# Last group of the FFN: three quarters stored over SyncE's and GpSimd's queues, and the last product ordered by token halves

## Chip, cores and metric

The kernel runs on one core of a Trainium2 chip. The metric is the device time of one execution in microseconds. The kernel before takes 313.97 us, the median of three runs (313.96 to 314.85). The profiled execution of it spans 312.5 us from its first to its last instruction, with a granted TensorE clock of 0.999.

## What is computed

A linear attention with cosine weights, then a SwiGLU feed-forward block. Cut to what matters:

```python
# q, k, v: 8 batches x 8 heads x 576 positions x 64
q_p, k_p = phi(q), phi(k)            # relu, times cos and sin of the position: 128 features
num = q_p @ (k_p^T @ v);  den = q_p . sum(k_p) + 1e-6
x = (num / den) as 4608 tokens x 512
out = (silu(x @ w_gate) * (x @ w_val)) @ w_out      # d_ff = 1536, out 4608 x 512, float32
```

## The kernel before

The 4608 tokens go through the feed-forward block in nine groups of 512 (`NTG` = 9, groups 0 to 8). Within a group, the gate and value products fill `ht`, the hidden activations (128 x 12 x 512, fp16), and then `out_by_quarters` (L818) multiplies `ht` by `w_out`. The order of the work is written out by hand (`manual_schedule`): each engine runs its instructions in the order in which they stand in the program, and semaphores hold an instruction until its inputs are there.

**The output product.** `out_by_quarters` computes the 512 x 512 output of a group as four quarters (C11, C12, C21, C22: 256 tokens by 256 columns each) by a scheme with seven products in place of eight. `product` (L835) is one of these: 12 matmuls of 128 x 256, over six blocks `kc` of the contraction and two halves `i` of 128 tokens. In the kernel before, `kc` is the outer loop, so that the two halves alternate and end one matmul apart. In the last group the running sum `b` lies in two PSUM banks, one for each half (`nb = 2 if last else 1`, L856); the helper `copied` (L849) then makes one VectorE instruction for each half. The order at the end of the last group is:

- `product(a, ..)` ends quarter C11; ScalarE scales and copies it into `ob` (L852); `store_two(t0, ..)` (L876).
- `product(b, S1, T1)` ends C22; VectorE adds it into `ob` in two instructions, one for each half (L880); `store_two(t0 + 2, ..)` (L882).
- `product(c, .., T4)` ends C21; ScalarE copies it (L852); `store_two(t0 + 2, ..)` (L887).
- `product(b, S4, ..)` ends C12, the last; VectorE copies it in two instructions (L854); `store` (L896) for each of the two token halves.

**The stores.** `store_two` (L765) writes one quarter with two transfers of 128 KB: `e = 0`, the lower 64 partitions, from SyncE, and `e = 1`, the upper 64, from ScalarE. The last quarter is written by `store` (L759) with four transfers of 64 KB, again one from SyncE and one from ScalarE for each half. Groups 1 to 7 store from GpSimd's queue alone (`queues`, L821). ScalarE issues no transfer anywhere in the kernel ahead of the first `store_two` of the last group. A transfer is issued from its engine's own instruction stream, so what stands behind it on that engine waits until the issue is over.

**The end.** Behind the last instruction (all of it has line L1148), SyncE waits for the semaphore of each transfer that is still counted, one instruction after the other. Every engine runs a DRAIN and reports; GpSimd collects the reports and releases all engines. Two such rounds close the program.

Of the kernel before, what the change touches and what calls it, by code (L numbers as in the profile page):

```python
# [18 lines left out]
def kernel(  # L19
# [10 lines left out]
    nc = tc.nc  # L30
    B, H, S, D = q.shape
    P = 128
# [15 lines left out]
    HC = FC // 2  # L48
# [38 lines left out]
    def take(n, hold=None, fills=False, seeded=False):  # L87

        taken = {x for r in held.values() for x in r}
        if loose[0]:  # L90
            free = [b for b in range(8) if b not in taken]
            if n == 1:
                bs = [min((b for b in free if filled[b] or not seeded), key=lambda b: used[b])]
            else:
                b0 = min((b for b in free if b + 1 in free), key=lambda b: max(used[b:b + 2]))
                bs = [b0, b0 + 1]
            if hold is not None:
                held[hold] = bs
            for b in bs:
                filled[b] = fills or seeded  # L100
            touch(bs)
            return banks[:, bs[0]] if n == 1 else banks[:, bs[0]:bs[0] + 2]
        free = [b for b in range(0, 8, n) if not any(b <= x < b + n for x in taken)
                and (filled[b] or not seeded)]

        b0 = min(free, key=lambda b: (n == 1 and hold is not None and hold[0] == "o" and b ^ 1 not in taken,
                                      sorted(used[b:b + n], reverse=True)))
        if hold is not None:
            held[hold] = range(b0, b0 + n)
        filled[b0:b0 + n] = [fills or seeded] * n  # L110
        touch(range(b0, b0 + n))
        return banks[:, b0] if n == 1 else banks[:, b0:b0 + n]
# [10 lines left out]
    def give_back(hold, late=1):  # L123
        touch(held.pop(hold), late)
# [32 lines left out]
    def lodge(n, dt):  # L157
        o = taken_up[0]
        taken_up[0] += n * (2 if dt == FP32 else 1)
        assert taken_up[0] <= 4 * HC * HD  # L160
        part = spare[:, o:taken_up[0]]
        return part if dt == FP16 else part.bitcast(dt)

    first = {"q": lodge(G * QCUT * D, FP32).rearrange("p (g c d) -> p g c d", g=G, c=QCUT)}
# [40 lines left out]
    def idle_products(n, cols=P):  # L205
# [37 lines left out]
        out=tab.rearrange("p c e d -> p (c e) d"),  # L243
# [508 lines left out]
    def ob_of(t):  # L752

        h, i = divmod(t, 2)
        if h not in obs:
            obs[h] = obp.tile([P, 2, d_model], FP32, name="ob")
        return obs[h][:, i]

    def store(t, cols=slice(0, d_model), queues=None):  # L759
        for e in range(2):  # L760
            idx = 2 * t + e
            (queues or (nc.sync, nc.sync))[e].dma_start(out=out_v[idx // NC, idx % NC][:, cols],  # L762
                                                        in_=ob_of(t)[e * SH:(e + 1) * SH, cols])

    def store_two(t, cols):  # L765
        for e in range(2):
            (b, c), (b1, _) = divmod(2 * t + e, NC), divmod(2 * t + 2 + e, NC)
            assert b == b1
            (nc.sync, nc.scalar)[e].dma_start(
                out=out_v[b, c:c + 3:2, :, cols].rearrange("c p f -> p c f"),  # L770
                in_=obs[t // 2][e * SH:(e + 1) * SH, :, cols])

# [21 lines left out]
    bq = wo_sb.rearrange("p (i w) (h x) -> p w h i x", w=2, h=2)  # L794
    sums = consts.tile([P, 3, HC, HT], FP16, name="sums")
    S1, S2, S3, S4 = aq[:, 0, 1], sums[:, 0], sums[:, 1], sums[:, 2]
# [7 lines left out]
    def token_sum(n, lo, hi):  # L804
        o, x, y, op = {
            3: (S3, aq[:, 0, 0], aq[:, 0, 1], ALU.subtract),
            1: (S1, aq[:, 0, 1], aq[:, 1, 1], ALU.add),
            2: (S2, S1, aq[:, 0, 0], ALU.subtract),
            4: (S4, aq[:, 1, 0], S2, ALU.subtract),
        }[n]  # L810
        nc.vector.tensor_tensor(out=o[:, lo:hi], in0=x[:, lo:hi], in1=y[:, lo:hi], op=op)
# [6 lines left out]
    def out_by_quarters(tg, slot_of):  # L818

        last = tg == NTG - 1  # L820
        queues = (nc.gpsimd, nc.gpsimd) if tg > 0 else None  # L821
        t0 = tg * OUT
        for t in (t0, t0 + 2):
            ob_of(t)
        C11, C12 = (obs[t0 // 2][:, :, x * HD:(x + 1) * HD] for x in range(2))
        C21, C22 = (obs[t0 // 2 + 1][:, :, x * HD:(x + 1) * HD] for x in range(2))

        def home(nm, parts=1, **kw):
            return [take(1, ("o", tg, nm, i), **kw).rearrange("p (t x) -> p t x", x=HD) for i in range(parts)]

        def free(nm, parts=1):
            for i in range(parts):
                give_back(("o", tg, nm, i))

        def product(to, a, b, first):  # L835
            rows[0] += LATE["O"]
            for kc in range(HC):
                for i in range(2):
                    nc.tensor.matmul(out=to[i][:, 0] if len(to) == 2 else to[0][:, i],  # L839
                                     lhsT=a[:, kc, i * P:(i + 1) * P], rhs=b[:, kc],  # L840
                                     start=first and kc == 0 and i == 0,
                                     stop=kc == HC - 1, skip_group_check=True)

        def each(ps, *others):
            if len(ps) == 1:
                return [(ps[0], *others)]
            return [(ps[i][:, 0:1], *(o[:, i:i + 1] for o in others)) for i in range(2)]

        def copied(eng, o, ps, x=DOWN):  # L849
            for p_, o_ in each(ps, o):  # L850
                if eng == "act":
                    nc.scalar.mul(out=o_, in_=p_, mul=x)  # L852
                else:
                    nc.vector.tensor_single_scalar(out=o_, in_=p_, scalar=x, op=ALU.mult)  # L854

        nb = 2 if last else 1  # L856
        a = home("a", fills=True)
        product(a, aq[:, 0, 0], bq[:, 0, 0], True)
        b = home("b", nb, seeded=True)
        for p_, o_ in each(b, a[0]):  # L860
            nc.scalar.copy(out=p_, in_=o_)
        e = home("e", fills=True)
        product(e, S3, T3, True)
        nc.scalar.mul(out=C22, in_=e[0], mul=DOWN)
        c = home("c", seeded=True)
        free("e")
        product(b, S2, T2, False)
        for p_, o_, x_ in each(b, c[0], C22):
            nc.vector.scalar_tensor_tensor(out=o_, in0=x_, scalar=UP, in1=p_, op0=ALU.mult, op1=ALU.add)
        token_sum(4, 0 if tg in GATE else 4, 6)  # L870
        slot_of(0)
        product(a, aq[:, 1, 0], bq[:, 1, 0], False)
        copied("act", C11, a)
        free("a")
        if last:
            store_two(t0, slice(0, HD))  # L876
        slot_of(1)
        product(b, S1, T1, False)
        for p_, x_ in each(b, C22):
            nc.vector.scalar_tensor_tensor(out=x_, in0=p_, scalar=DOWN, in1=x_, op0=ALU.mult, op1=ALU.add)  # L880
        if last:
            store_two(t0 + 2, slice(HD, d_model))  # L882
        product(c, aq[:, 1, 1], T4, False)
        copied("act", C21, c)
        free("c")
        if last:
            store_two(t0 + 2, slice(0, HD))  # L887
        else:
            for t in (t0 + 2, t0 + 3):
                store(t, queues=queues)  # L890
        slot_of(2)
        product(b, S4, bq[:, 1, 1], False)
        copied("dve", C12, b)
        free("b", nb)
        for t in (t0, t0 + 1):
            store(t, *((slice(HD, d_model), (nc.sync, nc.scalar)) if last else (slice(0, d_model), queues)))  # L896
        slot_of(3)
# [63 lines left out]
    halves = (slice(0, KC // 2), slice(KC // 2, KC))  # L961
    for word in words:
        word, _, eng = word.partition("@")
        op, a, b = re.match(r"([A-Za-z]+)(\d+)\.?(\d*)", word).groups()
        whole, a, part = b not in ("0", "1") or a != "0", int(a), int(b or 0)
# [187 lines left out]
```

## Time and profile before

| what | value |
| --- | --- |
| time, median of 3 | 313.97 us |
| span of the profiled execution | 312.5 us |
| TensorE busy with matmuls | 303.3 us, 97% of the span |
| VectorE, ScalarE, GpSimd busy | 235.9, 154.7, 66.0 us |
| share of L839 (products of `out_by_quarters`) on the chain that ended last | 21% |
| last matmul of the program starts | 306.6 us |
| last transfer issued | 309.0 us, from ScalarE |
| end of the span | 312.5 us |

TensorE is busy from end to end, so up to 306.9 us only its own work sets the time. The change lies in the last nine microseconds, of which the last 5.6 have no matmul: copies, stores, their landing, and the closing rounds. The shares of busy time over the whole span say nothing on this stretch; it is read from the timeline of the last ten microseconds and from the groups of the lines L769, L762 and L1148.

### The profile page before, as it was taken

What the parts mean: (1) busy time and instruction counts of PE and PEld (TensorE: products, weight loads), DVE (VectorE), ACT (ScalarE), POOL (GpSimd) and SP (SyncE); (2) the same over time, 40 slices, a digit from 0 to 9 for tenths busy, and PEclk for the clock granted to TensorE, in tenths of its full rate; (3) what the DMA queues carried; (4) which work ended last, traced back from release to release, by engine and by line L of the source; (5) the groups of instructions that cost most, each with busy time, mean ns of one, the idle gap of its engine ahead of it and who ended that gap; (6) DMA issues with size and microseconds to landing.
All of it is one profiled execution on the core that took longest, in us unless ns stands there. A gap on an engine that the chain in (4) does not pass through costs nothing.

```text
span 312.5 us, 6945 instructions
## 1 busy us (share of the span) xinstructions
PE 303.3 (97%) x2768; PEld 196.9 (63%) x2768; DVE 235.9 (75%) x474; ACT 154.7 (49%) x294; POOL 66.0 (21%) x118
## 2 busy tenths in 40 slices
PE   8799999999999999999999999999999999999992
PEld 3587465445445486547654686768767876786682
DVE  7774678787876988587887887898789569855771
ACT  7454556673435446435545454778543344334520
POOL 7754202001420405030413031202200220040000
PEclk9999999999999999999999999999999999999999
DMA  7999999998798898979496979790991141022005
GB/s 257 222 198 196 206 205 128 236 134 111 115 235 125 137 186 142 167 107 202 84 187 90 200 124 197 79 149 19 169 135 33 23 131 36 20 63 71 2 1 134
DMA packets 72976, 41.08 MB, mean 131 GB/s; under 512 B 49904, under 2 KB 69872, under 8 KB 72944
## 3 DMA queue, kind: packets, MB, share of 16 engines
q0 software_dynamic: 24880, 24.91, 46.6%
q1 hardware_dynamic: 47472, 15.21, 30.8%
q10 hardware_dynamic: 592, 0.52, 0.6%
q8 instruction: 21, 0.34, 0.4%
q14 instruction: 11, 0.09, 0.1%
HBM read 37.75 MB, written 9.44 MB: 151 GB/s over the span
## 4 chain that ended last, share of the span: by engine, by line
PE 92%; DMA 3%; DVE 2%; SPq 1%; ACT 1%; issue 0%; DVEq 0%; ACTq 0%
PE banks L605 33%; PE banks L839 21%; PE banks L676 13%; PE banks L663 11%; PE banks L780 6%; PE banks L354 3%; DMA ht<-in_k_dram 3%; PE banks L485 2%; PE banks L535 1%; SPq L171 1%; PE banks L466 1%; DVE ht L681 1%; PE banks L577 0%; DVE x L512 0%; ACT phit L417 0%
## 5 line engine op out<-in xcount | busy, mean ns | idle before, releaser
L611 ACT ACTIVATE sg<-banks 128x512 bf16<-128x512 f32 (+2 forms) x68 | 37.2, 548 | 52.4 <-PE banks L605 49.9
L605 PE MATMUL banks<-xT,wg_sb 128*128 128x512 f16 (+2 forms) x272 | 62.0, 354 | 0.0
L605 PE MATMUL banks<-xT,wv_sb 128*128 128x512 f16 (+2 forms) x272 | 62.0, 354 | 0.0
L616 DVE TENSOR_TENSOR ht<-sg,banks 128x512 f16<-128x512 bf16 (+2 forms) x68 | 41.7, 622 | 21.9 <-PE banks L605 15.4
L762 POOL DMA_DIRECT2D out_dram<-ob x56 | 29.5, 534 | 116.8 <-ACT ob L852 111.2
L676 PE MATMUL banks<-xT,wv_sb 128*128 128x512 f16 x192 | 48.6, 379 | 0.0
L605 PEld LDWEIGHTS <-wv_sb 128*128 128x128 f16 x272 | 26.1, 98 | 26.1
L605 PEld LDWEIGHTS <-wg_sb 128*128 128x128 f16 x272 | 24.8, 98 | 21.5
L839 PEld LDWEIGHTS <-ht 128*128 128x128 f16 x336 | 32.8, 98 | 4.8
L681 DVE TENSOR_TENSOR ht<-sg,banks 128x512 f16<-128x512 bf16 x48 | 31.0, 681 | 3.3 <-ACT sg L669 3.3
L676 PEld LDWEIGHTS <-wv_sb 128*128 128x128 f16 x192 | 18.8, 98 | 13.3
L839 PEld LDWEIGHTS <-sums 128*128 128x128 f16 x252 | 24.7, 98 | 2.9
L669 ACT ACTIVATE sg<-banks 128x512 bf16<-128x512 f32 x36 | 20.5, 590 | 11.8 <-PE banks L663 11.8
L780 PE MATMUL banks<-wo_sb,ht 128*128 128x512 f16 x96 | 22.7, 379 | 0.0
L512 DVE TENSOR_TENSOR x<-banks,rec 128x512 f16<-128x512 f32 (+1 forms) x32 | 21.6, 674 | 1.3 <-PE banks L466 0.3
L663 PEld LDWEIGHTS <-wgs_sb 128*128 128x128 f16 x192 | 17.8, 98 | 7.4 <-issue 0.6
L663 PE MATMUL banks<-kvt,wgs_sb 128*128 128x256 f16 x144 | 21.6, 273 | 0.4 <-DVE x L512 0.4
L839 PE MATMUL banks<-wo_sb,ht 128*128 128x256 f16 x168 | 20.6, 273 | 0.0
L304 DVE TENSOR_TENSOR v<-raw_v,tab 128x1152 bf16<-128x1152 bf16 x27 | 19.8, 753 | 0.3 <-ACT raw_v L902 0.3
L839 PE MATMUL banks<-wt_sb,sums 128*128 128x256 f16 x168 | 19.5, 273 | 0.0
L839 PE MATMUL banks<-wt_sb,ht 128*128 128x256 f16 x168 | 19.5, 273 | 0.0
L852 ACT ACTIVATE ob<-banks 128x512 f32<-128x512 f32 x14 | 8.4, 598 | 22.1 <-PE banks L839 19.0
(125 smaller groups left out, 409.0 us busy)
## 6 DMA issues: line engine op xcount, KB each, us to landing
out_dram<-ob POOLq DMA_DIRECT2D x56, 128.0 KB, 4.1
raw_k<-in_k_dram POOLq DMA_DIRECT2D x7, 576.0 KB, 6.0
raw_q<-in_q_dram POOLq DMA_DIRECT2D x6, 576.0 KB, 11.3
raw_v<-in_v_dram POOLq DMA_DIRECT2D x6, 576.0 KB, 9.3
wo_sb<-in_moe_w_out_dram POOLq DMA_DIRECT2D x3, 512.0 KB, 12.8
out_dram<-ob SPq DMA_DIRECT2D x11, 128.0 KB, 5.8
wg_sb<-in_moe_w_gate_dram POOLq DMA_DIRECT2D x5, 256.0 KB, 9.1
wv_sb<-in_moe_w_val_dram POOLq DMA_DIRECT2D x5, 256.0 KB, 9.6
```

The source lines that it names most:

```text
L304: nc.vector.tensor_tensor(out=v2s[b == 1][:, g, :, :, 0:D], in0=(first if b == 0 and g == 0 else {"v": raw_of(b, "v")})["v"][:, g].unsquee ...
L512: nc.vector.tensor_tensor(out=st["x", t].rearrange("p (y e d) -> p e y d", e=2, d=D)[:, :, ys], in0=ps[:, :, 0:2 * J * D1].rearrange("p e ...
L605: nc.tensor.matmul(out=st["f", tg, fc, lo][i], lhsT=(wg_sb, wv_sb)[i][:, kc, fs], rhs=xT[tg][:, ts, kc], start=(kc == 0), stop=(kc == KC - 1))
L611: nc.scalar.activation(out=sg[:, 0:n], in_=st["f", tg, fc, lo][0], func=AF.Silu, scale=DOWN)
L616: nc.vector.tensor_tensor(out=ht[:, fc, r:r + n], in0=st.pop(("s", tg, fc, lo))[:, 0:n], in1=ps[1], op=ALU.mult)
L663: nc.tensor.matmul(out=to[:, i], lhsT=a[:, c, 2 * u + i], rhs=x[:, :, c], start=first and i == 0 and c == 0, stop=c == KH - 1, skip_group_ ...
L669: nc.scalar.activation(out=gates[u, w][:, :, j * HT:(j + 1) * HT], in_=src, func=AF.Silu, scale=DOWN)
L676: nc.tensor.matmul(out=val[u, i, w], lhsT=wv_sb[:, kc, fc * P:(fc + 1) * P], rhs=xT[tg][:, :, kc], start=(kc == 0), stop=(kc == KC - 1))
L681: nc.vector.tensor_tensor(out=ht[:, fc], in0=gates[u, w][:, i], in1=val.pop((u, i, w)), op=ALU.mult)
L762: (queues or (nc.sync, nc.sync))[e].dma_start(out=out_v[idx // NC, idx % NC][:, cols], in_=ob_of(t)[e * SH:(e + 1) * SH, cols])
L780: nc.tensor.matmul(out=o_ps[t], lhsT=ht[:, fc, r:r + P], rhs=wo_sb[:, fc], start=(fc == 0), stop=(fc == FC - 1))
L839: nc.tensor.matmul(out=to[i][:, 0] if len(to) == 2 else to[0][:, i], lhsT=a[:, kc, i * P:(i + 1) * P], rhs=b[:, kc], start=first and kc == ...
```

## The change

Three edits, all of which act in the last group alone. First, `store_two` issues the upper halves of C11, C22 and C21 from GpSimd and no longer from ScalarE. This takes the issue of these transfers out of ScalarE's stream, in which the copy of C21 stands behind two of them. Second, `product` gets an argument `halves`: the 12 matmuls are sorted by `i`, so that all six of the first token half come ahead of the six of the second. Third, the last product is called with it, so that the first half of C12 can be copied and stored while TensorE still works on the second. The stores of the last quarter stay on SyncE and ScalarE.

```diff
         for e in range(2):
             (b, c), (b1, _) = divmod(2 * t + e, NC), divmod(2 * t + 2 + e, NC)
             assert b == b1
-            (nc.sync, nc.scalar)[e].dma_start(
+            (nc.sync, nc.gpsimd)[e].dma_start(
                 out=out_v[b, c:c + 3:2, :, cols].rearrange("c p f -> p c f"),
                 in_=obs[t // 2][e * SH:(e + 1) * SH, :, cols])
...
-        def product(to, a, b, first):
+        def product(to, a, b, first, halves=False):
             rows[0] += LATE["O"]
-            for kc in range(HC):
-                for i in range(2):
-                    nc.tensor.matmul(out=to[i][:, 0] if len(to) == 2 else to[0][:, i],
-                                     lhsT=a[:, kc, i * P:(i + 1) * P], rhs=b[:, kc],
-                                     start=first and kc == 0 and i == 0,
-                                     stop=kc == HC - 1, skip_group_check=True)
+            steps = [(kc, i) for kc in range(HC) for i in range(2)]
+            for kc, i in sorted(steps, key=lambda x: x[1]) if halves else steps:
+                nc.tensor.matmul(out=to[i][:, 0] if len(to) == 2 else to[0][:, i],
+                                 lhsT=a[:, kc, i * P:(i + 1) * P], rhs=b[:, kc],
+                                 start=first and kc == 0 and i == 0,
+                                 stop=kc == HC - 1, skip_group_check=True)
...
-        product(b, S4, bq[:, 1, 1], False)
+        product(b, S4, bq[:, 1, 1], False, last)
```

## The prediction

> **What bounds the kernel now.** I read the chain of waits first: 92% of it is TensorE, and its last pieces are the products of L839 up to 306.79, then one VectorE copy. So the edits can gain only behind the last matmul. The timeline of the last microseconds, in three windows (start, length, engine, line), shows that stretch:
>
> ```profile
> 303.61 0.66 SPq L769 DMA_DIRECT2D out_dram<-ob  x1
> 303.62 2.36 ACTq L769 DMA_DIRECT2D out_dram<-ob  x1
> ...
> 306.08 0.62 ACTq L769 DMA_DIRECT2D out_dram<-ob  x1
> 306.28 0.60 PE L839 MATMUL banks<-wo_sb,sums 128*128 128x256 f16 x4
> 306.50 0.10 PEld L839 LDWEIGHTS <-sums 128*128 128x128 f16 x1
> 306.74 0.60 ACT L852 ACTIVATE ob<-banks 128x512 f32<-128x512 f32 x1 [3.15 <-issue]
> 306.81 0.76 DVE L854 TENSOR_SCALAR ob<-banks 128x256 f32<-128x256 f32 x2 [1.87 <-PE banks L839]
> 307.37 0.60 SPq L769 DMA_DIRECT2D out_dram<-ob  x1
> 307.37 0.64 ACTq L769 DMA_DIRECT2D out_dram<-ob  x1
> ...
> 308.06 1.20 SPq L762 DMA_DIRECT2D out_dram<-ob  x2
> 308.10 1.45 ACTq L762 DMA_DIRECT2D out_dram<-ob  x2
> ```
>
> ScalarE's first transfer holds its stream for 2.36 us, where SyncE's at the same moment holds it for 0.66. The second follows at 306.08, and only then comes ScalarE's copy of C21 at 306.74. Its product had its last matmul at 305.30; C11's copy started 0.31 us behind its last matmul (302.68 to 302.99), so C21's could have started at 305.61. It is 1.13 us late, and with it both queues: the last four stores, ready at 307.57, go out behind it, the last from ScalarE at 309.00. That one lands 2.2 us later, at 311.2.
>
> What follows is the close (L1148), read from its group in two windows, 270 to 300 and 309 to 313 (columns: count, shortest/median/longest ns, first and last start):
>
> ```profile
> L1148 POOLq DRAIN  x1: 6733/6733/6733, 280.9 to 280.9; - x1
> ...
> L1148 SPq EVENT_SEMAPHORE  x11: 17/28/28, 309.3 to 312.5; - x11
> L1148 POOLq EVENT_SEMAPHORE  x4: 17/17/17, 311.8 to 312.4; - x4
> L1148 SPq DRAIN  x3: 7/7/13, 311.7 to 312.0; - x3
> L1148 ACTq DRAIN  x2: 8/202/396, 309.6 to 312.0; - x2
> ```
>
> From the landing (311.17 to the hundredth) SyncE needs 0.5 us for its other waits, GpSimd collects the reports at 311.78, and the two rounds take 0.74 us to 312.52. The line to keep is GpSimd's DRAIN of 6.73 us. It begins at 280.94 while the stores of group 7 are issued, and ends at 287.67. It costs nothing now, since GpSimd has no work in the last 24 us. The change puts work there.
>
> **What the Trainium skill says.** "Perfetto Trace Analysis", section on the HWDGE DMA instruction, says that the profiled span of an issue runs until the sequencer is free again and holds none of the data movement; the trace agrees: issues of 0.6 us, landings at 2.2 to 2.5. "DMA: Bandwidth & Descriptors", section on the anatomy of a DMA on the GpSimd path, fits 2.0 us plus bytes / 436 GB/s; for 128 KB, by my estimate from it, 2.3 us. The first of group 7's stores landed in 2.3, the last two of the eight in 2.9 to 3.0. "VectorE: DVE Perf Modes", section "The DRAIN you can't avoid", puts the DRAINs of preamble and postamble at about 12 ns on all five engines. GpSimd's here, behind transfers, took 6733 ns, and the measurement decides.
>
> **The change, part by part.**
>
> 1. ScalarE without stores. C21's copy starts at 305.61 and ends at 306.21 (0.60 as now), 1.13 us sooner. SyncE's half of C21 goes out at 306.24 (0.03 behind the copy, as at 303.61) and holds SyncE until 306.84. The earlier SyncE stores are unchanged.
> 2. TensorE runs the same 12 matmuls at 0.109 us from start to start, with the same weight loads: cost nothing. The sixth starts at 305.41 + 5 x 0.109 = 305.96 instead of the eleventh at 306.50. VectorE's copy of the first half starts 0.31 behind, at 306.27, and ends at 306.69. The second half's starts at 306.61 + 0.31 = 306.92 and ends at 307.34 (now 307.57, since it stood behind the first): a gain of 0.23.
> 3. SyncE's part of C12 then goes out at 306.89 and 307.50 (0.56 each, 0.05 between) and lands at 309.8 (2.3).
> 4. ScalarE's part of C12. Its first transfer of the program is now the first half of C12, at 306.72. The excess of 2.36 - 0.64 = 1.7 us was not lock or traffic: SyncE issued at the same time in 0.66, and in the window 303.7 to 304.6 the DMA view shows one packet of 8 KB on an instruction queue, 0.4 us behind the start. I take it as the cost of ScalarE's first issue, so it moves to the worst place. Bounds: 0 if it belonged to something else, 1.7 if to the first issue; I take 1.7. Then ScalarE is held to 309.08, the second half goes out at 309.13 and lands at 311.3 (2.2): no better than 311.2 now. The 1.4 us won in steps 1 to 3 are given back.
> 5. GpSimd. Three stores of 128 KB, at C11, C22 and C21. In group 7, GpSimd issued 0.29 behind the end of ScalarE's copy (277.51 to 277.80), so C21's starts at 306.21 + 0.29 = 306.50. Such a store had 64 rows and took 0.53; with 256 rows (the loads of two parts) 0.70 to 0.71; for 128 rows I take 0.59, so it ends at 307.09. Behind it stands GpSimd's DRAIN, and behind that the collecting of reports, for which every engine waits.
> 6. The DRAIN. The trace shows it once, so its law is open. It ended 5.70 us behind the end of the last issue (281.97), or 3.26 behind the last landing (284.41). Lower bound: the 0.05 to 0.10 us of the DRAINs at the end, with nothing outstanding. If it counts from the issue, GpSimd is ready at 307.09 + 5.70 = 312.79; if from the landing, at 306.50 + 2.6 + 3.26 = 312.36 (2.6 lies between 2.3 and 3.0). Both are later than 311.78. I take the first, because the DRAIN overlaps the landing anyway and nothing shows that it waits for one.
>
> **Sum:** GpSimd ready at 312.79 plus 0.74 for the rounds gives a span of 313.53, which is 1.0 more than 312.52: 315.0 us. All that the other edits bring lies in the shadow of this DRAIN.
>
> **Rivals.**
>
> - *DRAIN counted from the landing.* 312.36 + 0.74 = 313.10, +0.6: 314.5 us. For it: a drain that waits for transfers is what the name suggests. Against it: 3.26 us behind a landing still need a cause.
> - *DRAIN short, ScalarE's first issue long.* The 6.7 us could belong to eight stores in a row; for three, 3/8 of 5.70 is 2.1 us, over at 309.2. Then the last landing at 311.3 sets the end. Before, it was followed by 1.36 us, of which up to 0.5 are other waits that drop out if this transfer's semaphore is waited for last: 312.2 to 312.7, a time of 313.7 to 314.1, no change. For it: the 8 KB packet. Against it: the eight stores were issued every 0.52 us and landed without a growing delay beyond 0.7, so no backlog of descriptor work was left to drain.
> - *Neither cost appears.* ScalarE issues at 306.72 and 307.45, all is landed at 309.8 to 310.1 (these transfers now overlap C21's), and the end comes 0.93 to 1.36 later: 310.7 to 311.5, or 312.2 to 312.9 us, faster. For it: both costs were seen once only. Against it: each has its own line in the profile, and both have to be absent.
>
> **How the numbers follow.** DRAIN from the issue 0.50, from the landing 0.17, first issue alone 0.15, neither 0.18. The predicted time is that of the first, 315.0. The bound of slower by 0.3% is 314.91, close to it: with an issue of 0.53 to 0.71 us the first case reaches from 314.9 to 315.1, so I give 0.38 of its 0.50 to slower and 0.12 to no change; of the second 0.03 and 0.14; of the third 0.14 to no change and 0.01 to faster; the fourth is faster. Sums: slower 0.41, same 0.40, faster 0.19. The range starts at 312.8, just within the fast case's slow end, and reaches to 315.5, which adds the spread of single runs to the first case's 315.1.
>
> **What would show it.** The profile after should have ScalarE's copy of C21 near 305.6, the first copy of L854 near 306.3, and one ScalarE issue of about 2.4 us at line L762 near 306.7. GpSimd's DRAIN should begin near 306.5 and end near 312.8, with the first of its closing semaphores at 312.8 and not at 311.8, and SyncE's last wait over earlier than that. I am wrong if that DRAIN ends before SyncE's last wait, or if ScalarE's first issue takes 0.6 us; both together mean faster.

## The result, and the profile after

The changed kernel takes 315.68 us (median of six runs, 315.42 to 315.97), against 314.18 for the kernel before (six runs, 313.96 to 314.85). The ratio is 1.0043, with a 95% interval of 1.0031 to 1.0056: slower, by 1.0 to 1.8 us. I had forecast slower, with 315.0 us; the measured time is 0.7 us above that and 0.18 above the end of the range. The profiled execution spans 313.66 us, 1.14 more than before.

The timeline of the last microseconds, in three windows (start, length, engine, line, operation; in brackets the idle time ahead and what ended it):

```profile
303.43 0.66 SPq L769 DMA_DIRECT2D out_dram<-ob  x1
303.70 0.61 POOL L769 DMA_DIRECT2D out_dram<-ob  x1 [21.92 <-ACT ob L852]
...
305.43 0.60 ACT L852 ACTIVATE ob<-banks 128x512 f32<-128x512 f32 x1 [2.02 <-PE banks L839]
306.08 0.42 DVE L854 TENSOR_SCALAR ob<-banks 128x256 f32<-128x256 f32 x1 [1.32 <-PE banks L839]
...
306.32 0.60 POOL L769 DMA_DIRECT2D out_dram<-ob  x1 [0.65 <-ACT ob L852]
306.54 1.32 ACTq L762 DMA_DIRECT2D out_dram<-ob  x2
306.74 0.42 DVE L854 TENSOR_SCALAR ob<-banks 128x256 f32<-128x256 f32 x1 [0.23 <-PE banks L839]
306.74 1.30 SPq L762 DMA_DIRECT2D out_dram<-ob  x2
```

What the change was made for has come. ScalarE's copy of C21 starts at 305.43 and not at 306.74, the first copy of C12 at 306.08, and the last store goes out at 307.39 and not at 309.00. This execution reached the last group 0.18 us sooner (first store at 303.43, before 303.61), so 1.1 us of the 1.3 at C21's copy are the change's own.

The group of the closing line L1148, in the window from 306 to 312 and then from 306.5 to the end (count, shortest/median/longest ns, first and last start):

```profile
L1148 SPq EVENT_SEMAPHORE  x9: 28/28/967, 308.1 to 310.0; - x9
L1148 SPq DRAIN  x2: 7/10/13, 310.1 to 310.1; - x2
L1148 POOLq DRAIN  x1: 6573/6573/6573, 306.3 to 306.3; - x1
...
L1148 POOLq EVENT_SEMAPHORE  x4: 17/17/17, 312.9 to 313.6; - x4
```

SyncE has waited for every store by 310.0 and reports at 310.14, 1.6 us sooner than before (311.75). Then nothing happens until GpSimd's DRAIN of 6.57 us ends at 312.87; its first semaphore, which collects the reports, stands at 312.91 and no longer at 311.78. The two closing rounds follow. Counted from SyncE's report, GpSimd's DRAIN held the end for 2.7 us. SyncE's table of waits says the same: its wait in the close (the instructions of L1148) for another engine's part of the barrier had 0.5 us as its longest before (first line: us in total, times, longest), and 2.9 now (second line).

```profile
SPq L1148 <- PEq L1148: 0.7, 2, 0.5
...
SPq L1148 <- PEq L1148: 3.4, 2, 2.9
SPq L1148 <- DMA out_dram<-ob: 1.5, 4, 1.0
```

The label of these lines names TensorE, whose DRAIN had long been over (1.92 us from 304.83): a wait for several engines is put down to the wrong one here. The engine that was late is found in the group of L1148.

### The profile page after: what moved, and what is told of

Same layout as the page of the kernel before. It is cut to its first block, busy times and chain, and to the rows that moved or that the text cites. A ratio compares the mean times of both kernels' runs of the same rounds, so it can differ in the third digit from the quotient of the medians.

```text
span 313.7 us, 6946 instructions
## 1 busy us (share of the span) xinstructions
PE 304.0 (97%) x2768; PEld 197.1 (63%) x2768; DVE 235.8 (75%) x474; ACT 154.3 (49%) x294; POOL 67.9 (22%) x121
## 4 chain that ended last, share of the span: by engine, by line
PE 89%; DVE 5%; DMA 2%; ACT 2%; issue 0%; DVEq 0%; ACTq 0%
PE banks L605 32%; PE banks L839 18%; PE banks L676 13%; PE banks L663 11%; PE banks L780 6%; PE banks L354 3%; PE banks L485 2%; DMA xT<-x 2%; PE banks L535 1%; PE banks L466 1%; DVE x L512 1%; DVE v L304 1%; DVE ht L616 1%; DVE ht L681 1%; DVE sums L811 1%; PE banks L208 1%
```

## The experiments

The theory is that GpSimd's DRAIN behind its last transfer sets the end. The rivals: the order by halves costs; the DRAIN is a fixed thing that has nothing to do with the stores; ScalarE's first issue sets the end. The last of these falls in the trace above: ScalarE's first issue took 0.56 us, and the last store of all had landed (its semaphore told that it was done) at 309.93, 2.9 us before the DRAIN ended. Where a trace is quoted, it is that of the profiled execution. From one such execution to the next, the first store of the last group went out anywhere from 303.2 to 304.2 us in kernels with the same work ahead of it, so lengths from that store on are compared, not clock times.

**The order by halves alone (halves_only).**

```diff
-            (nc.sync, nc.gpsimd)[e].dma_start(
+            (nc.sync, nc.scalar)[e].dma_start(
```

> The change with its first edit undone: the upper halves of C11, C22 and C21 go from ScalarE again, the last product runs by halves. Theory (GpSimd's closing DRAIN is what made the change slower): no GpSimd work at the end, so its DRAIN ends near 288 us. ScalarE's first issue of 2.36 us still stands ahead of the copy of C21, and the last four stores still go out behind C21's at about 308.0, so the 0.55 and 0.23 us that the copies of C12 win are lost in that queue: about 314.2 us, as before. Rival (the order by halves itself is what costs): about 315.7, as the change.

Measured: 314.08 us, ratio to the kernel before 0.9993 (0.9983 to 1.0002). As the theory has it. ScalarE's issue at C11 took 2.42 us, C21's copy came late again, and the last store went out at 309.50. The order by halves costs nothing that these runs can tell, and brings nothing while this queue stands in front of it.

**The queues alone (queues_only).**

```diff
-        product(b, S4, bq[:, 1, 1], False, last)
+        product(b, S4, bq[:, 1, 1], False)
```

> The change with its second and third edit undone: GpSimd has the upper halves of three quarters, the last product alternates its halves as before. DRAIN theory: GpSimd's last issue ends at about 306.9 as in the change, its DRAIN at 312.8 to 312.9, and the span 0.79 us later: about 315.7 us, as the change. Rival (the order by halves costs): about 314.2.

Measured: 315.41 us, ratio 1.0034 (1.0024 to 1.0043). As far as the intervals tell, the whole slowdown lies in the first edit. GpSimd's DRAIN is the same to the nanosecond:

```profile
L1148 POOLq DRAIN  x1: 6573/6573/6573, 306.3 to 306.3; - x1
```

**No GpSimd store in the last group (no_gpsimd).** `store_two` gets its queue as an argument:

```diff
-    def store_two(t, cols):
+    def store_two(t, cols, upper):
-            (nc.sync, nc.gpsimd)[e].dma_start(
+            (nc.sync, upper)[e].dma_start(
-            store_two(t0, slice(0, HD))                    # C11
+            store_two(t0, slice(0, HD), nc.sync)
-            store_two(t0 + 2, slice(HD, d_model))          # C22
+            store_two(t0 + 2, slice(HD, d_model), nc.sync)
-            store_two(t0 + 2, slice(0, HD))                # C21
+            store_two(t0 + 2, slice(0, HD), nc.scalar)
```

> The change with no GpSimd store in the last group: SyncE takes both halves of C11 and C22, ScalarE the upper half of C21. DRAIN theory: GpSimd's DRAIN ends near 288. The issues on SyncE follow each other at about 0.65 us and end near 307.9, the last landing is at 310.0 to 310.2, and 0.9 to 1.1 us later the span ends, at 311.0 to 311.2: about 312.7 us, faster than both kernels. Rival 1 (ScalarE's first issue takes 2.36 us after all): its part of C12 goes out at 308.4 and 309.0 and lands at 311.2, about 314.0. Rival 2 (the DRAIN is not the cause): 315.7.

Measured: 313.09 us, ratio 0.9957 (0.994 to 0.9973): faster than the kernel before, and by the medians 2.6 us below the changed one, close to the 2.7 us for which the DRAIN held the end there. I had expected 312.7. The group of L1148, in the windows 279 to 300 and 300 to 312:

```profile
L1148 POOLq DRAIN  x1: 6720/6720/6720, 280.6 to 280.6; - x1
...
L1148 POOLq EVENT_SEMAPHORE  x4: 17/17/17, 310.6 to 311.2; - x4
L1148 SPq DRAIN  x3: 7/7/7, 310.5 to 310.8; - x3
```

The DRAIN of 6.72 us is back behind group 7, where nobody waits for it, and GpSimd's first semaphore now follows SyncE's report within 0.03 us: the transfers set the end again. SyncE, with five 128 KB stores in a row, 0.65 to 0.71 us from one to the next, is not too slow for it. ScalarE's first issue, now at C21, took 0.75 us. This undoes the cause and the effect goes: it is the strongest of the runs.

**Fewer GpSimd stores at the end (gpsimd_two, gpsimd_one).** On no_gpsimd (the comments tell which kernel has the line):

```diff
-            store_two(t0, slice(0, HD), nc.sync)
+            store_two(t0, slice(0, HD), nc.gpsimd)                # both kernels
-            store_two(t0 + 2, slice(HD, d_model), nc.sync)
+            store_two(t0 + 2, slice(HD, d_model), nc.gpsimd)      # gpsimd_two alone
```

> The change with the upper half of C21 on ScalarE, so that GpSimd stores the upper halves of C11 and C22 alone. DRAIN counted from the end of the last issue (5.7 to 5.95 us): that issue ends at 305.67 instead of 306.92, so the DRAIN ends at 311.4 to 311.6, 1.25 us sooner than in the change, and the span at 312.2 to 312.4: about 314.3 us. DRAIN counted from the landing (3.3 to 3.8): it ends at 311.0 to 311.5, about 313.9 to 314.2. A DRAIN that takes longer with more transfers (three in the change): it ends at 309.6 to 311, and the span with the last landing at 311.0 to 311.8: about 313.

> GpSimd stores the upper half of C11 alone; SyncE takes both halves of C22, ScalarE the upper half of C21. DRAIN counted from the last issue (5.87 to 5.95 us in the runs so far): the issue starts about 1.36 us sooner than C22's and ends at about 305.0 on the clock of the run with two, so the DRAIN ends there near 310.9, and about 2.65 us sooner than in the change. That is at about the time when SyncE's last wait ends, so the span is that of the kernel without GpSimd plus at most 0.4 us: 313.1 to 313.5 us. If the DRAIN takes longer with each transfer (6.57 us with three, 6.50 with two), it takes 6.43. Rival (a fixed time at which GpSimd becomes free whatever it issued last): 314.3 or more.

Measured: with two, 314.33 us, ratio 0.9996 (0.9986 to 1.0006); with one, 312.86, ratio 0.9958 (0.9942 to 0.9974).

GpSimd's last store and its DRAIN, with two and then with one:

```profile
305.76 0.61 POOL L769 DMA_DIRECT2D out_dram<-ob  x1 [0.75 <-DVE ob L880]
L1148 POOLq DRAIN  x1: 6500/6500/6500, 305.7 to 305.7; - x1
...
304.45 0.61 POOL L769 DMA_DIRECT2D out_dram<-ob  x1 [21.93 <-ACT ob L852]
L1148 POOLq DRAIN  x1: 6420/6420/6420, 304.4 to 304.4; - x1
```

With two, the DRAIN ends 1.5 us behind SyncE's report (312.24, 310.75) and sets the end still. With one, it ends 0.3 us ahead of it (310.85, 311.14) and costs nothing. So the DRAIN moves with GpSimd's last issue, and where it is over before the transfers, the loss is gone. The rival of a fixed time falls.

**Issue or landing (late_load).** On no_gpsimd, two loads that nobody reads are added; a small copy on GpSimd makes them wait until C11 is in place:

```diff
+            nc.gpsimd.tensor_copy(out=hold, in_=C11[:, 0, 0:1])
+            for nm in ("k", "v"):
+                load(B - 1, nm)
```

> The kernel without GpSimd stores in the last group, with two loads of 576 KB added on GpSimd once C11 is in place (they read k and v of the last batch again, into buffers that nobody reads any more; the result is not touched). Each of them lands several us behind its issue. Both issues are over at about 305.5. DRAIN counted from the last issue: it ends 5.7 to 6.0 us behind it, near 311.4, whether or not the loads have landed. DRAIN counted from the last landing: it ends 3.3 to 3.8 us behind that, at 313 or later. The end of the span tells nothing here, since the loads also delay the stores and are waited for; the DRAIN's own end is read.

```profile
304.52 0.77 POOL L142 DMA_DIRECT2D raw_v<-in_v_dram  x1
...
DMA to landing us min/median/max: 7.3/9.4/11.5
...
L1151 POOLq DRAIN  x1: 14827/14827/14827, 304.2 to 304.2; - x1
```

The timeline, the landing of both loads, and the DRAIN. The last issue is over at 305.29, the second load has landed at 304.52 + 11.5 = 316.05, and the DRAIN ends at 319.00: 13.7 us behind the issue and 2.9 behind the landing (I had expected 5.7 to 6.0 or 3.3 to 3.8). So a slow transfer does hold it, against the law that I took. This is one execution, and its time (321.57 us) says nothing on the stores, which the loads delay too. Landing alone is no law either. In prime_sync and prime_scalar (below), the last GpSimd store landed 2.60 and 2.24 us behind the end of its issue, and the DRAIN ended 5.62 us behind that issue in both. For the stores of these kernels, which land in 2 to 3 us, it counts from the issue.

**How long (merged, split_loads).** In the other runs, the time from the end of the last issue to the end of the DRAIN was 5.62 us where GpSimd had issued 98 transfers in the whole program, then 5.70 (99, in five kernels), 5.79 (100), 5.87 (101) and 5.95 (102, in two). Each step is 0.082. So two kernels change the number in the earlier groups and leave the last one alone. merged writes two tiles of the same batch with one transfer in groups 2 to 7, at two places of which the first is shown (`store_pair` is a new helper):

```diff
-            for t in (t0 + 2, t0 + 3):
-                store(t, queues=queues)
+            store_pair(t0 + 2, queues)       # one transfer for two tiles of one batch
```

split_loads cuts each of the 18 loads of batches 2 to 7 in two:

```diff
+        parts = 2 if b > 1 else parts
         t, sv, n = raw_of(b, nm), source(b, nm), G // parts
```

> The change, with 17 fewer GpSimd transfers earlier in the program: in groups 2 to 7 the stores of two token tiles go in one transfer where both lie in the same batch (85 in all, not 102). The last group is untouched. Behind 98, 99, 100, 101 and 102 transfers of the whole program the DRAIN ended 5.62, 5.70, 5.79, 5.87 and 5.95 us behind the last issue: 0.082 us more with each. Theory (its length goes with the transfers of the whole program): 5.95 - 17 x 0.082 = 4.55 us behind the last issue, and 1.4 us off the time: about 314.2. Rival (only what is issued in the last microseconds counts, or it is fixed): 5.95 again, about 315.6.

> The change, with each of the 18 loads of batches 2 to 7 cut into two transfers of half its size, so 120 transfers on GpSimd and not 102. Theory (0.082 us for each transfer of the whole program): the DRAIN ends 5.95 + 18 x 0.082 = 7.43 us behind the last issue, and the time is about 317.1. Rival: 5.95 again, about 315.6, or a little more if the loads come late.

Measured: merged 314.81 us, ratio 1.0018 (1.001 to 1.0025); split_loads 316.78, ratio 1.0078 (1.0057 to 1.0098). GpSimd's last store and its DRAIN in merged, then in split_loads:

```profile
307.20 0.60 POOL L769 DMA_DIRECT2D out_dram<-ob  x1 [0.65 <-ACT ob L862]
L1159 POOLq DRAIN  x1: 5185/5185/5185, 307.2 to 307.2; - x1
...
306.52 0.61 POOL L770 DMA_DIRECT2D out_dram<-ob  x1 [0.65 <-ACT ob L853]
L1149 POOLq DRAIN  x1: 7638/7638/7638, 306.5 to 306.5; - x1
```

The DRAINs end 4.56 and 7.01 us behind the end of the last issue. For 17 fewer transfers the count gave 4.55, and that is met; for 18 more it gave 7.43, and only 1.06 of the 1.48 us came, 0.059 for each added load. So the DRAIN pays for transfers long past, more than 20 us after they landed, and for their number, since both kernels move the bytes that the changed one moves; the rival (only the last ones count) falls. The price of each isn't one constant: 0.082 where stores were added or taken away, 0.059 where loads were cut in two; why it differs is open. merged won 0.9 us on the changed kernel where 1.4 were expected. In its trace the last group began late (first store at 304.32 us); from that store to the end it took 8.95 us, against 10.23 in the changed kernel, so 1.3 of the 1.4 us came in the close, and the rest of the time is not explained.

**What the order by halves is worth (no_gpsimd_alternating).** On no_gpsimd:

```diff
-        product(b, S4, bq[:, 1, 1], False, last)
+        product(b, S4, bq[:, 1, 1], False)
```

> The kernel without GpSimd stores in the last group, with the two token halves alternating in the last product as before. This tells what the order by halves is worth once neither a DRAIN nor ScalarE's long issue hides it. Theory: the copies of C12 end 0.57 and 0.23 us later, so the last stores go out about 0.2 to 0.5 us later: 313.2 to 313.6 us. Rival (the queues, not the copies, set when the last stores go out): 313.0, as with the order by halves.

Measured: 313.21 us, ratio 0.996 (0.9947 to 0.9973), against 0.9957 (0.994 to 0.9973) with the order by halves. The intervals cover each other: the order by halves is worth no more than these runs can tell. The last store went out 4.35 us behind the first store of the group here and 4.37 with the order by halves. In no_gpsimd its data were in place at 307.03, and it waited 0.64 us more for ScalarE's queue, which was issuing C21 and the first half of C12: what the copy wins, the queue takes in this trace.

**ScalarE's long issue (prime_sync, prime_scalar, c11_scalar).** Both primes are halves_only with one store of group 7 on another queue; of the changed line the new part is shown:

```diff
+   (nc.sync, nc.gpsimd) if tg == NTG - 2 and t == t0 + 1 else queues    # prime_sync
+   (nc.scalar, nc.gpsimd) if tg == NTG - 2 and t == t0 + 1 else queues  # prime_scalar
```

> The kernel with the order by halves and SyncE and ScalarE for the last stores, and one store of group 7 moved from GpSimd to SyncE. So SyncE has issued a plain transfer shortly ahead of the last group. Theory (ScalarE's long issue at C11 comes of SyncE's first plain transfer behind its transposes, beside which it stands): ScalarE's issue at C11 takes about 0.65 us instead of 2.4, the copy of C21 is over 1.1 us sooner, and the time is about 313.0. Rival (ScalarE's own first transfer is the long one, as the prediction had it): 2.4 us again, about 314.1.

> The same with that one store of group 7 on ScalarE in place of SyncE. Theory (it comes of SyncE's first plain transfer): ScalarE's issue at C11 still takes about 2.4 us, about 314.1. Rival (ScalarE's own first transfer): the store in group 7 takes 2.4 us and the issue at C11 about 0.65; about 313.0, if the wait in group 7 is hidden.

c11_scalar is no_gpsimd with both halves of C11 on ScalarE (`store_two` gets a queue for the lower half too; the call is shown):

```diff
-            store_two(t0, slice(0, HD), nc.sync)
+            store_two(t0, slice(0, HD), nc.scalar, nc.scalar)   # upper, lower
```

> The kernel without GpSimd stores in the last group, with both halves of C11 on ScalarE (SyncE has both of C22 and one of C21). ScalarE's first transfer of the program stands at C11 again, but no issue of SyncE beside it. Theory A (the 2.4 us come of standing beside an issue of SyncE): each issue takes 0.6 to 0.75 us, C21's copy is on time, about 313.0. Theory B (they come of ScalarE's first transfer where it follows a copy at this place): the first takes 2.4 us again, the second ends near 306.4, C21's copy is 1 us late, and the time about 314.

Measured: prime_sync 313.96 us, ratio 0.9993 (0.9985 to 1.0); prime_scalar 313.55, ratio 0.9981 (0.9973 to 0.999); c11_scalar 314.38, ratio 1.0003 (0.9993 to 1.0013). ScalarE's timeline from 303 us in prime_sync and c11_scalar, and from 278.5 in prime_scalar:

```profile
303.54 2.43 ACTq L769 DMA_DIRECT2D out_dram<-ob  x1
...
303.64 2.99 ACTq L769 DMA_DIRECT2D out_dram<-ob  x2
...
279.03 0.56 ACTq L762 DMA_DIRECT2D out_dram<-ob  x1
```

A transfer of SyncE ahead of it doesn't help, and in c11_scalar the first issue takes 2.20 of the 2.99 us with no issue of SyncE beside it: theory A falls. A transfer of ScalarE in group 7 does help: its issue at C11 then takes 0.68, and the median is 0.4 us below that of prime_sync, with intervals that overlap a little. (From C11's first store to the end its trace has 7.80 us, against 8.93 in prime_sync. This gain is larger than that in time, since the last group began later in it, at 304.10 and not at 303.54; whether the store in group 7 delays the group isn't shown.) But that transfer itself took 0.56, so it isn't simply that the first one is long. First transfers took 2.2 to 2.4 us in the four kernels that have them at C11, and 0.55 to 0.75 in the others, where they stand at C12, at C21 or in group 7. The 8 KB packet that I had built on is also seen 0.37 to 0.65 us behind C11's first store in kernels where ScalarE issues nothing there (no_gpsimd: packet at 303.67, store at 303.30), so it proves nothing. The cause of the long issue stays open.

## Why the prediction was right and wrong

- **Bound and direction: right.** The end was set by GpSimd's DRAIN; queues_only, no_gpsimd and gpsimd_one show it from three sides. I had been far from sure: this case had a chance of 0.50, and slower 0.41 against 0.40 for no change.
- **Steps 1 and 2: right.** C21's copy was to start 305.61 - 303.61 = 2.00 us behind C11's first store and did so (305.43 - 303.43); before it was 3.13. The copies of C12 started at 306.08 and 306.74 (forecast 306.27 and 306.92, less the 0.18 by which this execution was ahead).
- **Step 3: the landings too short.** I took 2.3 us for SyncE's two stores of C12; they landed after 2.79 and 2.54. My line that issues land after 2.2 to 2.5 us was too narrow for the trace of before as well: nine of its ten last stores took 2.2 to 2.9, and the one with the long issue 4.15. None of this cost the forecast anything, since the DRAIN ended later.
- **Step 4: wrong.** ScalarE's first issue was to take 2.36 us and move with the change. It took 0.56, at C12. It cost the forecast nothing, since it lay in the DRAIN's shadow, but the rival built on it had no ground. I had seen one long issue and one packet beside it, and taken the neighbour for the cause.
- **Step 5: right.** The last issue started 0.29 us behind ScalarE's copy and took 0.60 (forecast 0.29 and 0.59).
- **Step 6: right in kind, wrong as a law, and too small.** I took 5.70 us from the end of the last issue; it was 5.95. The missing 0.25 is three transfers more at 0.082. What I wrote as its reason, that nothing shows that the DRAIN waits for a landing, fell with late_load; so counting from the issue was right by luck, because these stores land in under 3 us. "VectorE: DVE Perf Modes" in the Trainium skill, section "The DRAIN you can't avoid", gives about 12 ns for the DRAINs of preamble and postamble. The closing DRAINs here carry the kernel's own line L1148, so that figure may not be meant for them, as I had taken it; GpSimd's lasted 5.2 to 7.6 us behind the stores of these kernels, and 14.8 behind the late loads.
- **Sum: the span nearly met, in part by luck.** Forecast 313.53, measured 313.66. The 0.13 are +0.25 (DRAIN), +0.05 (from the DRAIN's end to the end of the span 0.79 and not 0.74: GpSimd's first semaphore came 0.04 behind its DRAIN), -0.17 (last issue over at 306.92 and not at 307.09). The last of these is no merit of the forecast: this execution reached the last group 0.18 us sooner than the one before. From the first store of the last group to the end I had forecast 9.92 us (313.53 - 303.61); it was 10.23, where before it had been 8.91. So the change cost 1.32 us there and not 1.0.
- **From the span to the time: the step that failed most.** I added the span's gain, 1.0 us, to the median of before, 313.97. But the execution whose profile I had worked in was one of 314.31 us, 0.34 above that median. Its span plus the same 1.79 us (314.31 - 312.52) would have given 313.53 + 1.79 = 315.32. It was the median of three that lay low: the six runs beside the changed kernel have 314.18, and the sets of 31 to 41 runs in the experiments 314.10 to 314.32. With 314.18 and the 1.32 us the sum is 315.50. So two terms were too small, the time that I started from by 0.21 us and the close by 0.31, 0.25 of it the DRAIN. The 0.2 us that remain to 315.68 are within what the interval of the ratio leaves open (1.0 to 1.8 us slower), and no run explains them.

## What to carry to other kernels

Read the group of the closing instructions before work is put on an engine near the end: GpSimd's DRAIN was hidden before, but its length was in the profile, and it moved with GpSimd's last issue. Here a queue that lands a store in 2.7 us (SyncE: 2.6) cost 1.5 us, because its engine could report only 5.95 us after its last issue. In gpsimd_one the store from GpSimd was free, because the DRAIN behind it was over 0.3 us before SyncE had waited for the last landing; in the changed kernel it was over 2.7 us after that. And when a span is turned into a time, add the offset of the profiled run itself: a median of three runs that spread over 0.9 us was 0.2 us too low here.

## What the hardware showed that I had not expected

- GpSimd's closing DRAIN grew with the number of transfers that GpSimd issued in the whole program: it ended 4.56 us behind the last issue for 85, 5.62 to 5.95 for 98 to 102 (0.082 each), 7.01 for 120. Below 85 nothing was measured. Behind a load that landed late, 10.8 us after its issue was over, it ended 2.9 us after the landing.
- GpSimd began an issue 0.29 us behind the end of the ScalarE copy it waited for, SyncE 0.03 us behind it.
- The issue of ScalarE's first transfer took 2.2 to 2.4 us at one place of the program and 0.55 to 0.75 at three others; the cause is open.
- The kernel that is faster than both, no_gpsimd (313.09 us; gpsimd_one, 312.86, is as good within the intervals), needs none of the extra queue: SyncE alone issues five of the six 128 KB stores in time.
